# Two rows instead of nine: a narrower accumulator for the heads' sum in a decode step of sliding attention beside a gated unit

## The chip, the cores and the metric

The kernel runs on one core of a Trainium2 chip. The metric is the device time of one execution in microseconds; three runs of the kernel before gave a median of 377.54 us, from 377.41 to 377.73. The core has a matrix engine (TensorE, PE in the profile), a vector engine (VectorE, DVE), a scalar engine (ScalarE, ACT), a general engine (GpSimd, POOL) and a synchronisation engine (SyncE, SP), which here issues all DMA transfers. Sixteen DMA engines move the data between the chip's large memory and the on-chip memory SBUF. Matrix products land in a second small memory, PSUM.

## The reference

One token for each of two sequences (B = 2, D = 512) passes a layer norm, and the result feeds two branches whose outputs are added to the token: attention with 32 heads of width 128 over the last 2048 of 8192 cached positions, and a bilinear gated unit of width 1376.

```python
xn = _layernorm(x)
# attention, W = 2048
q = (xn @ wq).reshape(B, 1, 32, 128).transpose(0, 2, 1, 3)
scores = einsum("bhqd,bhkd->bhqk", q, k_cache[:, :, -W:]) * 128 ** -0.5
o = einsum("bhqk,bhkd->bhqd", softmax(scores), v_cache[:, :, -W:])
a = o.transpose(0, 2, 1, 3).reshape(B, 1, 4096) @ wo
# gated unit
b = ((xn @ w_gate) * (xn @ w_up)) @ w_down
return x + a + b
```

All values are float32. The keys, values and weights that are read make up nearly all of the 159.7 MB that the profile counts.

## The kernel before, in words

The host lays all large inputs out as one stream in the order of their use. The kernel reads it in 28 loads of up to 54 KB for each of the 128 partitions into three rotating buffers of SBUF (`step`, 55,296 bytes per partition), after one small load (`first`) with the token, two matrices of ones and zeros and the first head's query weights. The function `pump` issues a load as soon as a buffer is free; SP carries the loads out in this order and waits ahead of each for whatever used the buffer. An object `InOrder` ties each engine's instructions to the order in which the kernel names them.

For each head the keys lie with 16 positions of both sequences in each partition. DVE multiplies them with the broadcast query (`products`) and sums over the width (`sums`), POOL and ACT turn the sums into weights (`maxima`, `weights`), and PE multiplies the weights with the values (`weigh`), 16 columns wide in four column groups. ACT copies the result out, PE brings the head's output into a column for each sequence (`transpose`), and ACT scales it by the reciprocal of the sum into `oT`, a tile of 128 partitions by M columns.

The output product (`project_o`) then takes `oT` as the stationary operand and adds its product with the head's 128x512 slice of `wo` into the PSUM tile `acc`. The stationary operand has M = RB * (B - 1) + 1 = 9 columns, with the two sequences in columns 0 and 8 and zeros between (RB = 8). So the sums of the two sequences lie in rows 0 and 8 of `acc`. The gated unit uses the same layout: `gate` writes `hT` and `hX`, M columns wide at steps of RB, and `down` and `down_rest` add their products into the same rows.

Up to head 27 the whole 512 columns are one matmul. From head 28 on (`HF = H - 4`) the product is split into four column groups of 128 output columns each (`accumulate`), which land in rows 32g and 32g + 8 of a 128x128 view `acc_g`. Between the two, DVE copies the sum so far into SBUF (`acc_sb`, line 492), and `accumulate(carry, acc_sb)` brings it into the four groups by a matmul with the small matrix `carry`, which has ones at (0, 0) and (8, 8). At the very end DVE adds the token to the sums (line 529: `o_out` from `acc_g` and `x_nat`), and SP stores the 128x128 result, of which the host picks eight rows.

The token for that last addition comes by a load of 16 rows into `x_nat`, a 128x128 tile that a memset cleared ahead of it (lines 180 to 182), and `carry` comes by a load of 9 rows (line 185). Both are issued behind the first four loads of the stream. Memsets clear `oT`'s four copies (POOL, line 209), `hT` and `hX` (DVE, lines 391 and 394), since their columns between the two sequences must be zero.

Of the kernel before, what the change touches and what calls it, by code (L numbers as in the profile page):

```python
# [8 lines left out]
F32 = mybir.dt.float32  # L9
AF = mybir.ActivationFunctionType  # L10
ALU = mybir.AluOpType
# [5 lines left out]
P = 128  # L17
B, D, H, DH, SK, F = 2, 512, 32, 128, 8192, 1376
# [4 lines left out]
NFB = -(-F // FB)  # L23
NFC = F // P
FR = F - NFC * P
FH = [(0, 2 * FB), (2 * FB, F)]
LAG = 3
RB = 8
M = RB * (B - 1) + 1
OUT = P  # L30

CARRY = 72
HG = 4
GC = HG * DH
JG = J // 4
# [9 lines left out]
def blocks():  # L45

    def wd(n):
        return [("wd", i, D) for i in range(*WD[n])]

    def k(h):
        return [("k", h, CK)] + ([("wq", h, CP)] if h + HG < H else [])

    def v(h):  # L60
        return [("v", h, CK), ("wo", h, CO)]

    def gu(half):
        n = NC * (FH[half][1] - FH[half][0])
        return [("wg", half, n), ("wu", half, n)]

    units = []
    for h in range(LAG, H - 1):
        units += [k(h), v(h - LAG)]
    ones = [("pick", 0, 8 * B), ("rows", 0, NFB * B)]  # L70
    first = [("x", 0, B * NC)] + ones + [("w", 0, NC * DH)]
    loads = [[("w", 1, CQ - NC * DH)] + k(0) + k(1), gu(0) + k(2)]
    loads += [gu(1) + units[0] + units[1] + wd(0) + [("wr", 0, NS * P)]]
    loads += [sum(units[i : i + 3], []) for i in range(2, len(units), 3)]
    loads += [k(H - 1) + v(H - 1 - LAG) + wd(1)]
    out = [(("f", 0), first)] + [(("s", i), fields) for i, fields in enumerate(loads)]
    late, last = ("s", len(loads)), ("s", len(loads) + 1)
    out += [(late, v(H - 3)), (late, v(H - 2)), (last, [("v", H - 1, CK)])]
    out += [(last, [("wo", H - 1, CO)] + wd(2))]
    return out + [(last, wd(n)) for n in range(3, len(WD))]  # L80
# [33 lines left out]
def kernel(  # L114
    ctx: ExitStack,
    tc: tile.TileContext,
    x_rows: bass.AP,
    carry_rows: bass.AP,
    stream: bass.AP,
    out: bass.AP,  # L120
):
    nc = tc.nc
    pe, dve, act, sp = (InOrder(tc, e) for e in (nc.tensor, nc.vector, nc.scalar, nc.sync))
# [3 lines left out]
    const = ctx.enter_context(tc.tile_pool(name="const", bufs=1))  # L127
# [49 lines left out]
    pick = got["pick", 0][0].rearrange("p (r s b) -> p r s b", s=2, b=B)  # L177
    rows = got["rows", 0][0]

    x_nat = const.tile([P, P], F32, name="x_nat")  # L180
    dve.memset(x_nat, 0.0)
    sp.dma_start(x_nat[::RB, :], x_rows)

    carry = const.tile([P, CARRY], F32, name="carry")[:M, :M]
    sp.dma_start(carry, carry_rows)

    mean_w = const.tile([P, P], F32, name="mean_w")
    dve.memset(mean_w, 1.0 / D)
# [4 lines left out]
    dve.memset(acc_t, 0.0)  # L193
    acc, acc_g = acc_t[:M, :], acc_t[:, :P]

# [9 lines left out]


    oT_ring = [const.tile([P, M], F32, name=f"oT{i}") for i in range(4)]
    for t in oT_ring:
        nc.gpsimd.memset(t, 0.0)


    tr = ps_c.tile([P, 4 * P], F32, name="tr")
# [23 lines left out]
    q_ps, s_t, mm_t, p_t, sum_t, rec_t, o_sbs, oT = {}, {}, {}, {}, {}, {}, {}, {}  # L236
    n_acc = bank = 0

    def side(h):

        return int(h % 3 == 0)
# [43 lines left out]
    def sums(h):  # L285
        s_t[h] = small.tile([P, B, J], F32, name="s")
        dve.tensor_reduce(s_t[h], k_of(h), axis=AX.X, op=ALU.add)
        done("k", h)
# [28 lines left out]
    def accumulate(lhsT, rhs, last=False):  # L317
        nonlocal n_acc
        for g in range(4):
            pe.matmul(  # L320
                acc_g[32 * g : 32 * g + M, :], lhsT, rhs[:, g * P : (g + 1) * P],
                start=(n_acc == 0), stop=last,
# [23 lines left out]
    def transpose(heads, o_sb):  # L346
        d = tr[:, 8 + 4 * bank : 12 + 4 * bank]
        s0, s1 = side(heads[0]), side(heads[-1]) + 1
        dst = d.rearrange("p (s b) -> p s b", b=B)[:, s0:s1, :]
        for r in range(4):  # L350
            pe.matmul(
                dst, o_sb[:, r * DH : (r + 1) * DH], pick[:, r, s0:s1, :],
                start=(r == 0), stop=(r == 3),
            )
        for h in heads:
            rec = rec_t.pop(h)
            oT[h] = oT_ring[h % 4]
            for b in range(B):
                c = B * side(h) + b
                act.activation(  # L360
                    oT[h][:, RB * b : RB * b + 1], d[:, c : c + 1], AF.Copy,
                    scale=rec[:, b : b + 1],
                )

# [14 lines left out]
    def values(heads, busy=((), ())):  # L379
        o_sb = pv(heads)  # L380
        for n in busy[0]:
            keep_busy(n)
        transpose(heads, o_sb)
        for n in busy[1]:
            keep_busy(n)
        for h in heads:
            project_o(h)


    hT = const.tile([P, 4, NFB, M], F32, name="hT")  # L390
    dve.memset(hT, 0.0)

    hX = const.tile([P, NS, M], F32, name="hX")
    dve.memset(hX, 0.0)

    def project_gu(half):
        lo, hi = FH[half]
# [12 lines left out]
    def gate():  # L410
        g_sb = small.tile([P, FB], F32, name="o_sb", bufs=2)
        act.copy(g_sb, gu_ps[0])
        h_sb = small.tile([P, FB], F32, name="o_sb", bufs=2)
        dve.tensor_tensor(h_sb, g_sb, gu_ps[1], op=ALU.mult)
        for i in range(4):
            t = tr[:, P + i * P // 2 : P + i * P // 2 + NFB * B]
            pe.matmul(t, h_sb[:, i * P : (i + 1) * P], rows, start=True, stop=True)
            act.copy(hT[:, i, :, ::RB], t.rearrange("p (n b) -> p n b", b=B))
        for i in range(NS):
            t = tr[:, P + (2 * i + 1) * P // 4 : P + (2 * i + 1) * P // 4 + NFB * B]  # L420
            f = (NFC % 4) * P + i * FX - FR
            pe.matmul(t, h_sb[:, f : f + P], rows, start=True, stop=True)
            act.copy(hX[FR:, i, ::RB], t[FR:, (NFB - 1) * B :])

    def down(n):
        for c in range(*WD[n]):
# [51 lines left out]
    h = H - 2  # L478
# [10 lines left out]
    down(1)  # L489

    acc_sb = const.tile([M, D], F32, name="acc_sb")
    dve.tensor_copy(acc_sb, acc)
    sums(h + 1)
    transpose([HF], o_sb)
    keep_busy(256)
    accumulate(carry, acc_sb)
# [8 lines left out]
    o_sb = pv([H - 2])  # L505
    keep_busy(GC)
    transpose([H - 2], o_sb)
    keep_busy(256)
    project_o(H - 2)
# [3 lines left out]
    for k, t in enumerate((o_ps[bank], o_ps2)):  # L513
        for n in range(CK // FB):
            b, i = divmod(n, JG)
# [10 lines left out]
    down(3)  # L526
    down(4)
    o_out = const.tile([P, P], F32, name="o_out")
    dve.tensor_tensor(o_out, acc_g, x_nat, op=ALU.add)

    sp.dma_start(out, o_out[:OUT, :])

# [1 line left out]
def laid_out(x):  # L534

    import numpy as np

    a = x["A_x"].reshape(B, D)
    first = {
        kind: np.zeros((P, w), a.dtype) for kind, _, w in blocks()[0][1][:3]  # L540
    }
    carry = np.zeros((M, M), a.dtype)
    first["x"][:] = a.reshape(B, P, NC).transpose(1, 0, 2).reshape(P, B * NC)
    for b in range(B):
        for r in range(4):
            for s in range(2):
                first["pick"][8 * s + 4 * b + r :: 32, (2 * r + s) * B + b] = 1.0
        for n in range(NFB):
            first["rows"][32 * n + b, n * B + b] = 1.0
        carry[RB * b, RB * b] = 1.0  # L550
    cache = {
        kind: x[name][:, :, SK - W :, :].reshape(B, H, P, J * DH).transpose(1, 2, 0, 3)
        for kind, name in (("k", "A_k_cache"), ("v", "A_v_cache"))
    }
    wq = x["A_wq"].reshape(P, NC, H // HG, GC).transpose(2, 0, 1, 3)
    wo = x["A_wo"].reshape(H, P, D)
    gu = {
        kind: x[name].reshape(P, NC, F)
        for kind, name in (("wg", "B_w_gate"), ("wu", "B_w_up"))
    }  # L560
    wd = x["B_w_down"]
    rest = wd[NFC * P :].reshape(FR, NS + 1, P)

    def field(kind, i):
        if kind in first:
            return first[kind]
        if kind in ("k", "v"):
            return cache[kind][i].reshape(P, CK)
        if kind == "w":
            return (wq[0][:, :, DH:] if i else wq[0][:, :, :DH]).reshape(P, -1)  # L570
        if kind == "wq":
            return wq[i // HG + 1][:, i % HG, :]
        if kind == "wo":
            return wo[i]
        if kind == "wr":
            last = rest[:, NS, :].reshape(NS, FX, P).swapaxes(0, 1)
            return np.concatenate([rest[:, :NS, :], last]).reshape(P, NS * P)
        if kind == "wd":
            return wd[i * P : (i + 1) * P]
        return gu[kind][:, :, FH[i][0] : FH[i][1]].reshape(P, -1)  # L580

    parts = [
        np.concatenate([field(kind, i) for kind, i, _ in fields], axis=1).ravel()
        for _, fields in blocks()
    ]
    x_rows = np.zeros((D // P, 32 // RB, P), a.dtype)
    x_rows[:, :B] = a.reshape(B, D // P, P).transpose(1, 0, 2)
    return {
        "x_rows": x_rows.reshape(-1, P),
        "carry": carry,  # L590
        "stream": np.concatenate(parts),
    }

# [31 lines left out]
```

## Time and profile before

| what | value |
|---|---|
| median of three runs | 377.54 us (377.41 to 377.73) |
| span of the profiled execution, first to last instruction | 375.7 us |
| mean granted TensorE clock | 0.795 |
| PE, DVE, ACT, POOL busy | 68%, 78%, 16%, 7% |
| bytes moved by DMA, mean rate | 159.70 MB, 425 GB/s |

The profile is of one execution; it shows the span, and the time that the runs measure is somewhat longer, since it holds what lies around the first and the last instruction. Shares are of the span. In the rows of groups, the numbers behind the bar are busy time in all and the mean of one instruction, and behind the second bar the time in which the engine sat idle ahead of them and what ended it. Nearly all instructions carry line 98, the line of the helper that records their order, so that they are told apart by the names of their tiles. In the rows of the timeline the first number is the start in microseconds from the beginning of the span, the second the duration.

### The profile page before, as it was taken

How to read it: one execution, taken by the hardware profiler on the slowest of the kernel's cores; microseconds unless marked ns; L12 is line 12 of the kernel's file. 1: busy time of each engine (PE TensorE's matmuls, PEld its weight loads, DVE VectorE, ACT ScalarE, POOL GpSimd, SP SyncE). 2: the span in 40 equal slices, each digit the busy share in tenths (PEclk: the TensorE clock that was granted, in tenths of full speed). 3: DMA queues.
4: the chain of work that ended last, by engine and by line, in shares of the span. 5: the costliest groups of instructions: out<-in, count | busy, mean ns of one | idle time of the engine just before them, and what ended most of it. 6: DMA issues, size and time to landing. Idle time of an engine off the chain costs nothing.

```text
span 375.7 us, 2891 instructions
## 1 busy us (share of the span) xinstructions
PE 256.5 (68%) x1100; PEld 88.1 (23%) x1100; DVE 294.6 (78%) x147; ACT 58.7 (16%) x259; POOL 25.3 (7%) x78
## 2 busy tenths in 40 slices
PE   3396696986548487864848676485867639637996
PEld 3241122331112122211222211121212213021334
DVE  3299691998599499769949976994996799599960
ACT  1021001122020211201112020111202011121131
POOL 1001000000000000100000100000000000000010
PEclk9796988899696966859686786976669887556999
DMA  8999999899999999999999999999999999999995
GB/s 327 463 436 454 408 426 471 383 465 432 414 465 394 459 424 424 461 400 453 418 437 449 412 447 424 432 442 430 436 436 424 437 434 436 436 425 424 419 421 226
DMA packets 4382, 159.70 MB, mean 425 GB/s; under 512 B 514, under 2 KB 658, under 8 KB 1042
## 3 DMA queue, kind: packets, MB, share of 16 engines
q1 hardware_dynamic: 4370, 159.54, 98.5%
q8 instruction: 8, 0.13, 0.1%
q14 instruction: 4, 0.03, 0.0%
HBM read 159.47 MB, written 0.07 MB: 425 GB/s over the span
## 4 chain that ended last, share of the span: by engine, by line
DMA 62%; DVE 29%; PE 7%; ACT 1%; issue 0%; SPq 0%; DVEq 0%
DMA step<-in_stream_dram 62%; DVE s L98 14%; DVE step L98 14%; PE o_ps L98 3%; PE q L98 2%; PE acc L98 2%; PE tr L98 1%; DVE m L98 0%; ACT o_sb L98 0%; ACT oT L98 0%; SPq L98 0%; DVE rec L98 0%; DVE o_out L98 0%; DVEq L98 0%
## 5 line engine op out<-in xcount | busy, mean ns | idle before, releaser
L98 DVE TENSOR_TENSOR step<-step,q 128x4096 f32<-128x4096 f32 x31 | 136.6, 4408 | 53.3 <-DMA step<-in_stream_dram 53.3
L98 PE MATMUL q<-step,xnb 128*128 128x512 f32 (+1 forms) x128 | 92.7, 874 | 75.5 <-DMA step<-in_stream_dram 75.5
L98 DVE TENSOR_REDUCE s<-step 128x32 f32<-128x4096 f32 x32 | 141.4, 4419 | 1.1
L98 PE MATMUL o_ps<-step,p 128*16 128x512 f32 (+1 forms) x512 | 69.7, 682 | 10.3 <-DMA step<-in_stream_dram 10.3
L98 PEld LDWEIGHTS q<-step,xnb 128*128 128x128 f32 x128 | 32.2, 275 | 128.9 <-DMA step<-in_stream_dram 79.1
L98 PE MATMUL acc<-step,oT 128*9 128x512 f32 (+1 forms) x88 | 35.2, 554 | 9.3 <-ACT oT L98 8.1
L98 PE MATMUL tr<-first,o_sb 128*128 128x2 f32 (+2 forms) x198 | 27.6, 258 | 15.3 <-ACT o_sb L98 12.8
L98 ACT COPY o_sb<-o_ps 128x512 f32<-128x512 f32 (+1 forms) x24 | 13.8, 576 | 143.1 <-PE o_ps L98 143.1
L98 PEld LDWEIGHTS tr<-first,o_sb 128*128 128x128 f32 x198 | 25.5, 196 | 37.3 <-ACT o_sb L98 32.6
L295 POOL PARTITION_ALL_REDUCE mm<-m x32 | 11.3, 354 | 283.4 <-DVE rec L98 178.9
L98 PEld LDWEIGHTS o_ps<-step,p 128*16 128x16 f32 x512 | 13.5, 106 | 70.4 <-issue 55.2
L98 ACT ACTIVATE nm<-mm 128x2 f32<-128x2 f32 x32 | 6.5, 203 | 129.5 <-POOL mm L295 129.5
L98 ACT ACTIVATE p<-s,nm 128x16 f32<-128x16 f32 x64 | 19.2, 300 | 1.0
L98 ACT ACTIVATE oT<-tr,rec 128x1 f32<-128x1 f32 x64 | 12.2, 260 | 28.3 <-PE tr L98 28.3
L311 POOL PARTITION_ALL_REDUCE sum<-rs x32 | 12.7, 398 | 54.8 <-ACT p L98 54.8
L98 PE MATMUL o_ps<-step,xn 128*2 128x512 f32 (+1 forms) x48 | 12.9, 593 | 0.0
L98 ACT ACTIVATION_READ_ACCUMULATOR p<-s,nm 128x1 f32 x64 | 12.0, 187 | 0.0
L98 DVE TENSOR_TENSOR step<-step,tr 128x4096 f32<-128x4096 f32 x1 | 4.4, 4421 | 9.3 <-DMA step<-in_stream_dram 9.3
L98 PEld LDWEIGHTS acc<-step,oT 128*9 128x9 f32 x88 | 4.3, 91 | 19.5 <-ACT oT L98 13.1
L98 PE MATMUL q<-xnb,mean_w 128*128 128x512 f32 (+1 forms) x18 | 8.5, 563 | 0.0
L98 PE MATMUL acc<-step,hT 128*9 128x128 f32 (+2 forms) x58 | 7.9, 357 | 0.0
L98 DVE TENSOR_REDUCE m<-s 128x2 f32<-128x32 f32 x32 | 5.9, 186 | 1.1
(43 smaller groups left out, 36.5 us busy)
## 6 DMA issues: line engine op xcount, KB each, us to landing
step<-in_stream_dram SPq DMA_DIRECT2D x16, 6912.0 KB, 33.7
step<-in_stream_dram SPq DMA_DIRECT2D x2, 6400.0 KB, 32.6
step<-in_stream_dram SPq DMA_DIRECT2D x1, 6720.0 KB, 45.6
step<-in_stream_dram SPq DMA_DIRECT2D x1, 6656.0 KB, 28.9
step<-in_stream_dram SPq DMA_DIRECT2D x1, 5376.0 KB, 15.4
step<-in_stream_dram SPq DMA_DIRECT2D x1, 4864.0 KB, 30.1
step<-in_stream_dram SPq DMA_DIRECT2D x2, 2304.0 KB, 17.2
step<-in_stream_dram SPq DMA_DIRECT2D x1, 2048.0 KB, 15.9
```

The costliest lines, as they stand in the source:

```text
L98: made = call(*args, **kwargs)
L295: nc.gpsimd.partition_all_reduce(mm, m, P, bass_isa.ReduceOp.max)
L311: nc.gpsimd.partition_all_reduce(sum_t[h], rs, P, bass_isa.ReduceOp.add)
```

## The change

M becomes 2: the two sequences lie in rows 0 and 1 of `acc`, and in rows 32g and 32g + 1 of the four column groups. `oT`, `hT` and `hX` have two columns without gaps, and their memsets go. `x_nat` and `carry` become parts of one tile `x_own` of two rows, loaded at once: each row has a sequence's token (512 numbers) and a row of the 2x2 unit matrix. The token is added where the sum so far is carried over, on the 2x512 sum, and the last step on DVE is a copy.

```diff
-RB = 8
-M = RB * (B - 1) + 1
+M = B
@@
-    x_nat = const.tile([P, P], F32, name="x_nat")
-    dve.memset(x_nat, 0.0)
-    sp.dma_start(x_nat[::RB, :], x_rows)
-
-    carry = const.tile([P, CARRY], F32, name="carry")[:M, :M]
-    sp.dma_start(carry, carry_rows)
+    x_own = const.tile([P, D + M], F32, name="x_own")[:M, :]
+    sp.dma_start(x_own, x_rows)
+    x_nat, carry = x_own[:, :D], x_own[:, D:]
@@
     oT_ring = [const.tile([P, M], F32, name=f"oT{i}") for i in range(4)]
-    for t in oT_ring:
-        nc.gpsimd.memset(t, 0.0)
@@
-                    oT[h][:, RB * b : RB * b + 1], d[:, c : c + 1], AF.Copy,
+                    oT[h][:, b : b + 1], d[:, c : c + 1], AF.Copy,
@@
     hT = const.tile([P, 4, NFB, M], F32, name="hT")
-    dve.memset(hT, 0.0)
     hX = const.tile([P, NS, M], F32, name="hX")
-    dve.memset(hX, 0.0)
@@
-            act.copy(hT[:, i, :, ::RB], t.rearrange("p (n b) -> p n b", b=B))
+            act.copy(hT[:, i, :, :], t.rearrange("p (n b) -> p n b", b=B))
@@
-            act.copy(hX[FR:, i, ::RB], t[FR:, (NFB - 1) * B :])
+            act.copy(hX[FR:, i, :], t[FR:, (NFB - 1) * B :])
@@
-    dve.tensor_copy(acc_sb, acc)
+    dve.tensor_tensor(acc_sb, acc, x_nat, op=ALU.add)
@@
-    dve.tensor_tensor(o_out, acc_g, x_nat, op=ALU.add)
+    dve.tensor_copy(o_out, acc_g)
@@ on the host
-    x_rows = np.zeros((D // P, 32 // RB, P), a.dtype)
-    x_rows[:, :B] = a.reshape(B, D // P, P).transpose(1, 0, 2)
     return {
-        "x_rows": x_rows.reshape(-1, P),
-        "carry": carry,
+        "x_rows": np.concatenate([a, np.eye(M, dtype=a.dtype)], axis=1),
         "stream": np.concatenate(parts),
     }
```

More of the change, by code (lines that the diff above doesn't have):

```diff
@@ L27 @@
 LAG = 3
-RB = 8
-M = RB * (B - 1) + 1
+M = B
 OUT = P
-CARRY = 72
 HG = 4
@@ L117 @@
     x_rows: bass.AP,
-    carry_rows: bass.AP,
     stream: bass.AP,
@@ L541, in laid_out @@
     }
-    carry = np.zeros((M, M), a.dtype)
     first["x"][:] = a.reshape(B, P, NC).transpose(1, 0, 2).reshape(P, B * NC)
@@ L549, in laid_out @@
             first["rows"][32 * n + b, n * B + b] = 1.0
-        carry[RB * b, RB * b] = 1.0
     cache = {
@@ L623 @@
     y = r.results[0]["out_0_dram"]
-    return y[[32 * g + RB * b for b in range(B) for g in range(D // P)]].reshape(B, 1, D)
+    return y[[32 * g + b for b in range(B) for g in range(D // P)]].reshape(B, 1, D)
```

## The prediction

> **What bounds the kernel now.** I read the page first (engines, slices, queues, chain), then stretches of time, then the timeline of the head and of the tail.
>
> ```profile
> span 375.7 us, 2891 instructions
> PE 256.5 (68%) x1100; PEld 88.1 (23%) x1100; DVE 294.6 (78%) x147; ACT 58.7 (16%) x259; POOL 25.3 (7%) x78
> DMA  8999999899999999999999999999999999999995
> q1 hardware_dynamic: 4370, 159.54, 98.5%
> DMA 62%; DVE 29%; PE 7%; ACT 1%; issue 0%; SPq 0%; DVEq 0%
> step<-in_stream_dram SPq DMA_DIRECT2D x16, 6912.0 KB, 33.7
> first<-in_stream_dram SPq DMA_DIRECT2D x1, 271.0 KB, 2.9
> step<-in_stream_dram SPq DMA_DIRECT2D x1, 256.0 KB, 19.0
> ```
>
> No compute engine is busy over 78%, while one DMA queue is busy 98.5% of the span on all 16 engines. The chain of waits gives DVE 29%, but that is a habit of the view: it follows the buffer that the queue waited for, and the transfers went on beside it. The stretches of time tell whether they did; the last two columns are the busy share of the 16 DMA engines and the rate:
>
> ```profile
> 0.00:1.70 1.70, 0.00 (x0) 0.00 (x0) 0.78 (x4) 0.98 (x1) 1.17 (x14) 1.00 0.00 0
> 30.00:352.00 322.00, 220.43 (x842) 68.93 (x842) 266.69 (x119) 49.13 (x228) 21.83 (x58) 0.77 1.00 432
> 352.00:368.10 16.10, 15.79 (x120) 6.36 (x118) 10.66 (x10) 4.67 (x19) 1.50 (x4) 1.00 0.99 423
> 372.60:375.70 3.10, 0.35 (x8) 0.06 (x8) 0.29 (x1) 0.00 (x0) 0.00 (x0) 0.96 0.07 21
> ```
>
> For 322 us the share is 1.00 at 432 GB/s, although the TensorE clock was granted at 0.77 only. A load of 6912 KB (7.08 MB) at 432 GB/s takes 16.4 us but needs 33.7 us from issue to landing, so each load stands some 17 us in the queue behind another. That is the cover over everything PE, DVE, ACT and POOL do in the middle: an engine must be late by some 17 us before the queue runs dry. The end is set by the last rows of the stream and what follows them:
>
> ```profile
> 368.13 0.56 PEld L98 LDWEIGHTS o_ps<-step,p 128*16 128x16 f32 x16 [0.45 <-DMA step<-in_stream_dram]
> 372.55 0.12 PEld L98 LDWEIGHTS acc<-step,hT 128*9 128x9 f32 x8 [0.25 <-DMA step<-in_stream_dram]
> 373.02 0.29 DVE L98 TENSOR_TENSOR o_out<-acc,x_nat 128x128 f32<-128x128 f32 x1 [8.16 <-PE acc L98]
> 373.34 0.35 SPq L98 DMA_DIRECT2D out_dram<-o_out  x1
> ```
>
> PE sat idle 0.25 us for the last piece of weights, then 0.47 us until the sum was ready, 0.29 us on DVE, 0.03 to the issue, and 2.36 from there to the span's end. So the path is: 1.70 us before the first byte, the stream, and a tail of 3.15 us after 372.55. A change can move the time only by moving the stream's start, its rate or bytes, or one of those tail pieces. The span is 375.7; the three timed runs have their median 1.84 above it, and I carry that difference unchanged.
>
> **The change, part by part.**
>
> *Loads.* The head on SP and DVE:
>
> ```profile
> 0.82 0.17 DVE L98 MEMSET x_nat<- 128x128 f32 x1 [0.82 <-PEq L606]
> 1.15 1.37 SPq L98 DMA_DIRECT2D step<-in_stream_dram  x3
> 2.56 0.55 SPq L98 DMA_DIRECT2D x_nat<-in_x_rows_dram  x1
> 3.15 0.54 SPq L98 DMA_DIRECT2D carry<-in_carry_dram  x1
> 34.56 319.41 SPq L98 DMA_DIRECT2D step<-in_stream_dram  x25
> 3.64 0.16 DVE L98 TENSOR_REDUCE st<-first 128x2 f32<-128x8 f32 x1 [0.84 <-DMA first<-in_stream_dram]
> ```
>
> The stream's first four loads are issued before either small load, in both kernels. One issue of about 0.54 us goes from SP, which then has nothing to do from 3.69 to 34.56 us: worth 0. If that cover were gone it would be worth 0.54. The wait of the x load for a memset goes too, and nothing is queued behind it but the carry load. SP's later loads each wait for the load and the compute that used their buffer, in the same order; one load fewer only renumbers the completion semaphores.
>
> In the DMA queue itself the small loads stand between the third and the fourth buffer's load. Before: 16 rows of 512 B and 9 of 36 B; after: 2 rows of 2056 B. Prices come from stretches in which rows of one size only move (2168 B, 2048 B and 512 B, in this order):
>
> ```profile
> 2.32:2.82 0.50, 0.00 (x0) 0.00 (x0) 0.48 (x1) 0.00 (x0) 0.00 (x0) 1.00 0.84 330
> 371.36:371.76 0.40, 0.40 (x26) 0.38 (x19) 0.00 (x0) 0.24 (x2) 0.00 (x0) 1.00 0.48 184
> 374.18:374.45 0.27, 0.00 (x0) 0.00 (x0) 0.00 (x0) 0.00 (x0) 0.00 (x0) 1.00 0.78 231
> ```
>
> Rate over share, over 16 engines: 330/0.84/16 = 24.6 GB/s, so 88 ns for 2168 B; 184/0.48/16 = 24.0, so 85 ns for 2048 B; 231/0.78/16 = 18.5, so 28 ns for 512 B. An engine lost 28 to 56 ns before (a 36 B row costs between 0 and 28). After, an engine without a row loses nothing, and one with a row loses about 85. The stream ends with its slowest engine, which I can't name. Ends: -0.06 us (no row on that engine) and +0.14 (both rows on it: 170 - 28). I take -0.03, nearest to the 28 ns of the engines that had no 36 B row and now get nothing; that holds for most of the sixteen. The Trainium skill, page "DMA: Bandwidth & Descriptors", section "Why a DMA increments its semaphore by 16 and not by 1", says that a load is spread over the largest count up to 16 that divides its slowest dimension, so two rows would go to two engines; by it those two lose 85 ns and the sum would be +0.03 to +0.06 instead of -0.03. No run here shows it yet.
>
> *Memsets.* Removed:
>
> ```profile
> L209 POOL MEMSET oT<- 128x9 f32 x4 | 0.2, 107 | 0.0
> L98 DVE MEMSET hT<- 128x108 f32 x1 | 0.1, 148 | 0.0
> L98 DVE MEMSET hX<- 128x27 f32 x1 | 0.1, 81 | 0.0
> L98 DVE TENSOR_TENSOR step<-step,tr 128x4096 f32<-128x4096 f32 x1 | 4.4, 4421 | 9.3 <-DMA step<-in_stream_dram 9.3
> ```
>
> The x memset (0.17 us) lies ahead of 0.84 us idle for the first load, hT's and hX's (0.23) ahead of 9.3 us idle for the second, and POOL's 0.2 in front of nothing that is due before the first heads. Worth 0; without that cover 0.6 in all.
>
> *Width of the head sums, 9 columns to 2.* The matmul count stays. Rows for each width:
>
> ```profile
> L98 PE MATMUL acc<-step,oT 128*9 128x512 f32 x56 | 33.5, 714 | 9.3 <-ACT oT L98 8.1 <-ACT nm L98 1.2
> L98 PE MATMUL o_ps<-step,xn 128*2 128x512 f32 x32 | 8.0, 660 | 0.0
> L98 PEld LDWEIGHTS acc<-step,hT 128*9 128x9 f32 x56 | 1.9, 91 | 3.7 <-issue 3.4 <-DMA step<-in_stream_dram 0.3
> L98 PEld LDWEIGHTS o_ps<-step,xn 128*2 128x2 f32 x48 | 2.7, 88 | 11.6 <-issue 11.6
> ```
>
> A weight load is 3 ns shorter; the matmul means differ by 54 ns, but they come from stretches with other granted clocks, so the price of the width itself lies between 0 and 54. Ahead of the last load all of this is covered by the 17 us. After 372.55 there are eight pairs: four column groups at once, so at most two weight loads in a row, -0.01 to 0. ACT's copies into hT and hX and the scaled copies into oT keep their element counts and become contiguous; ACT is busy 16%: 0.
>
> *x joins the carried sum.* The 9x512 copy becomes an add of 2x512 from PSUM and SBUF:
>
> ```profile
> L98 DVE COPY acc_sb<-acc 9x512 f32<-9x512 f32 x1 | 0.7, 672 | 0.0
> L98 DVE TENSOR_TENSOR o_sb<-o_sb,o_ps 128x512 f32<-128x512 f32 x1 | 0.7, 678 | 0.0
> L98 DVE MEMSET x_nat<- x1: 165/165/165, 0.8 to 0.8; 128x128 f32 x1
> 363.30 0.13 PEld L98 LDWEIGHTS o_ps<-step,p 128*16 128x16 f32 x8 [0.46 <-DMA step<-in_stream_dram]
> ```
>
> By the add that the kernel already has, 678 against 672: +0.006 us at 356.80. Behind it on DVE stands the reduction of the last head, and PE waits for it with the carry matmuls; both then meet idle time for loads, 0.46 us at 363.30 and 0.45 at 368.13. The add now also waits for x, which comes before the fourth buffer's load, 300 us earlier. Worth 0, and 0.006 without the cover.
>
> *The last DVE step* loses an operand: add 292 ns to a copy from PSUM. The pair 672/678 says 6 ns; the outer ends are 165 (a memset of 128x128, which reads nothing) and 292. I take 0.286: -0.006, with -0.13 and 0 as ends. It lies wholly on the path.
>
> *Where the buffers lie.* The fixed tiles take 704 bytes more per partition, so in the built program's layout the three stream buffers start at 31424, 86720 and 142016 instead of 30720, 86016 and 141312 bytes: from multiples of 512 to odd multiples of 64. The stream is the bound, so even a few ns for each row would count: 28 loads x 128 rows / 16 engines = 224 rows per engine. The nearest row is the first load, which lies at 16512 (128 past a multiple of 256): its 2168 B took 88 ns against 85 for 2048 B at an aligned place, and 120 more bytes at 27 GB/s (432/16) are 4 ns. So nothing is charged for the place within the 1 to 2 ns of these figures. Ends: 0 and 7 ns per row; I take 0.
>
> Sum: -0.03 - 0.006 - 0.005 = -0.04 us; span 375.66, time **377.50**.
>
> **The rivals.**
>
> *A: the shifted buffers slow the stream (slower).* If an engine also moves the 192 bytes between the last 256-byte line and the start of each row, that is 192/27 = 7.1 ns x 224 = +1.6 us: 379.1. It decides from 3.4 ns a row (0.76 us). For it: the stream has no slack at all. Against it: the 88 ns of the first load, which would have been 93. The Trainium skill, page "DMA: Bandwidth & Descriptors", section "How a descriptor splits into AXI transactions", states for reads that a row not starting at a 256-byte boundary begins at the boundary below and pays for the unused bytes; applied to the writing side it would give the 379.1, and the first load's row does not bear it out. Chance 0.11.
>
> *B: the narrow width speeds up the path (faster).* If the buffers' release by PE were what paces the stream, the 64 matmuls of 512 columns would save up to 54 ns each, 3.4 us: 374.1. For it: the chain shows PE with 7%. Against it: share 1.00 at 432 GB/s over 322 us, which leaves nothing to speed up. Chance 0.05.
>
> *C: the merged load costs more than the two.* Both rows on the engine that ends last, +0.14 instead of -0.03: 377.67. For it: two long rows concentrate what sixteen short ones spread. It stays under what a measurement tells. Chance 0.15.
>
> **How the numbers follow.** My forecast has 0.67. It and C lie within 0.2% (0.76 us, about what a measurement of this kernel can tell from no change), 0.82 together. Slower: A and 0.01 for what I don't see, 0.12; faster: B and 0.01, 0.06. The forecast's own range: ends -0.2 and +0.2 and half the spread of the timed runs (0.16), 377.2 to 377.9. To leave no more than 2 in 10 out, with A at a part of its price, I reach to 377.0 and 378.2.
>
> **What would show it.** Right: 432 GB/s at share 1.00 in the middle; the first load of a buffer after the small one landing within 0.2 us of now; the last weights at 372.5; a last copy of 280 to 292 ns; the add at 670 to 685. A is seen in the rate of the middle stretch, below 431; B in narrower matmuls that end earlier and a last load that lands before 372 us; C in one engine's lag. The prediction is wrong if the rate moves, or if the tail after 372.55 is not 3.1 us.

## The result and the profile after

The changed kernel takes 378.19 us (median of 11 runs, 378.11 to 378.29) against 377.31 (11 runs) for the kernel before on the same chip: a ratio of 1.0020, 95% interval 1.0011 to 1.0029. It is slower by 0.88 us. My forecast was 377.50 and no change; the time lies just inside the stated range (377.0 to 378.2), outside the forecast's own 377.2 to 377.9, and the kernel got slower where I had forecast no change.

The page of the changed kernel, in the order of the prediction's first fence; the profiled execution took 378.21 us:

```profile
span 376.4 us, 2878 instructions
PE 256.4 (68%) x1100; PEld 88.4 (23%) x1100; DVE 294.4 (78%) x144; ACT 58.6 (16%) x259; POOL 25.2 (7%) x74
q1 hardware_dynamic: 4324, 159.54, 98.4%
step<-in_stream_dram SPq DMA_DIRECT2D x16, 6912.0 KB, 33.8
```

The engines' busy times hardly moved. The stretches of time (last columns: granted clock, DMA share, GB/s) say the same of the middle:

```profile
30.00:352.00 322.00, 218.05 (x839) 68.25 (x840) 266.38 (x119) 49.12 (x228) 21.84 (x58) 0.77 1.00 432
```

Both kernels read 432 GB/s here. That is no proof of equality: 0.88 us of 377 is 0.23%, and 0.23% of 432 is 1.0, which the whole numbers of this column can hide. The timeline shows what the rate can't. These are four of DVE's eleven multiplications that waited for a load, and for the changed kernel the tail from PE's last weights on; first the kernel before:

```profile
16.60 4.42 DVE L98 TENSOR_TENSOR step<-step,tr 128x4096 f32<-128x4096 f32 x1 [9.34 <-DMA step<-in_stream_dram]
97.97 4.42 DVE L98 TENSOR_TENSOR step<-step,q 128x4096 f32<-128x4096 f32 x1 [5.49 <-DMA step<-in_stream_dram]
228.41 4.42 DVE L98 TENSOR_TENSOR step<-step,q 128x4096 f32<-128x4096 f32 x1 [5.27 <-DMA step<-in_stream_dram]
325.15 4.42 DVE L98 TENSOR_TENSOR step<-step,q 128x4096 f32<-128x4096 f32 x1 [4.00 <-DMA step<-in_stream_dram]
```

and the changed kernel:

```profile
16.64 4.42 DVE L96 TENSOR_TENSOR step<-step,tr 128x4096 f32<-128x4096 f32 x1 [9.63 <-DMA step<-in_stream_dram]
98.04 4.42 DVE L96 TENSOR_TENSOR step<-step,q 128x4096 f32<-128x4096 f32 x1 [5.46 <-DMA step<-in_stream_dram]
228.76 4.42 DVE L96 TENSOR_TENSOR step<-step,q 128x4096 f32<-128x4096 f32 x1 [5.38 <-DMA step<-in_stream_dram]
325.60 4.42 DVE L96 TENSOR_TENSOR step<-step,q 128x4096 f32<-128x4096 f32 x1 [4.25 <-DMA step<-in_stream_dram]
373.20 0.11 PEld L96 LDWEIGHTS acc<-step,hT 128*2 128x2 f32 x8 [0.24 <-DMA step<-in_stream_dram]
373.67 0.29 DVE L96 COPY o_out<-acc 128x128 f32<-128x128 f32 x1 [7.99 <-PE acc L96]
373.99 0.35 SPq L96 DMA_DIRECT2D out_dram<-o_out  x1
```

The lag behind the kernel before is 0.04, 0.07, 0.35 and 0.45 us, and 0.65 at the last weights (372.55 before). So the loss builds up in the stream and was there before the tail began; each of these starts is from one execution, and those of two kernels of equal speed differ by up to 0.35 us (the first experiment). The tail from the last weights to the end is 3.2 us, as before. By 325 us all but 64 of each DMA engine's 224 rows are through (of the last eight loads seven are shorter): those 64 rows, 29%, fall into the last 47 us, an eighth of the time, and bring 0.20 of the 0.65. That hints at a lag that grows with rows rather than with time, but at this scatter it does not show it.

### The profile page after: what moved, and what is told of

Its sections match the earlier page's. It is cut to its first block, busy times and chain, and to the rows that moved or that the text cites. A ratio compares the mean times of both kernels' runs of the same rounds, so it can differ in the third digit from the quotient of the medians.

```text
span 376.4 us, 2878 instructions
## 1 busy us (share of the span) xinstructions
PE 256.4 (68%) x1100; PEld 88.4 (23%) x1100; DVE 294.4 (78%) x144; ACT 58.6 (16%) x259; POOL 25.2 (7%) x74
## 3 DMA queue, kind: packets, MB, share of 16 engines
q1 hardware_dynamic: 4324, 159.54, 98.4%
## 4 chain that ended last, share of the span: by engine, by line
DMA 62%; PE 20%; DVE 15%; ACT 1%; issue 1%; SPq 0%; DVEq 0%
DMA step<-in_stream_dram 62%; PE o_ps L96 8%; DVE s L96 7%; DVE step L96 7%; PE q L96 5%; PE acc L96 4%; PE tr L96 3%; ACT o_sb L96 0%; SPq L96 0%; ACT oT L96 0%; DVE o_sb L96 0%; ACT hT L96 0%; DVE m L96 0%; ACT hX L96 0%; DVE o_out L96 0%
## 5 line engine op out<-in xcount | busy, mean ns | idle before, releaser
L96 PE MATMUL acc<-step,oT 128*2 128x512 f32 (+1 forms) x88 | 35.0, 551 | 9.1 <-ACT oT L96 9.1
L96 PE MATMUL o_ps<-step,xn 128*2 128x512 f32 (+1 forms) x48 | 13.9, 615 | 0.0
L96 PEld LDWEIGHTS acc<-step,oT 128*2 128x2 f32 x88 | 3.8, 83 | 19.4 <-ACT oT L96 14.5
L96 DVE RECIPROCAL rec<-sum 128x2 f32<-128x2 f32 x32 | 5.0, 155 | 2.3 <-POOL sum L303 2.3
```

The source lines that it names most:

```text
L96: made = call(*args, **kwargs)
```

## The experiments

Theory D: the time goes into rows that are written to SBUF at places off some line, since the fixed tiles push the stream's buffers up by 704 bytes. Theory S: the stream lies at another place in the large memory, since the inputs ahead of it shrank. Theory L: the merged load, the narrower sums or another edit costs it.

**The changed kernel with its buffers moved back to multiples of 512.**

```diff
     hX = const.tile([P, NS, M], F32, name="hX")
+    pad = const.tile([P, 80], F32, name="pad")
+    nc.gpsimd.memset(pad[:, 0:1], 0.0)
```

> The changed kernel with 320 unused bytes ahead of the stream's buffers, so that these start at multiples of 512 again (31744, 87040, 142336). Theory D, the place of the buffers in SBUF slows the rows: back to the kernel before, 377.2 to 377.4 us, middle stretch back at 432 GB/s. Theory S, the place of the stream in the large memory moved because the inputs ahead of it shrank: still 378.1 to 378.3. Theory L, the merged load of two rows or another edit costs it: still 378.1 to 378.3.

Measured: 377.30 us against 377.40, ratio 0.9994 (0.9985 to 1.0004). All of the loss is gone, with every edit of the change in place. The same rows of its timeline:

```profile
16.45 4.42 DVE L96 TENSOR_TENSOR step<-step,tr 128x4096 f32<-128x4096 f32 x1 [9.46 <-DMA step<-in_stream_dram]
97.90 4.42 DVE L96 TENSOR_TENSOR step<-step,q 128x4096 f32<-128x4096 f32 x1 [5.70 <-DMA step<-in_stream_dram]
228.28 4.42 DVE L96 TENSOR_TENSOR step<-step,q 128x4096 f32<-128x4096 f32 x1 [5.33 <-DMA step<-in_stream_dram]
325.02 4.42 DVE L96 TENSOR_TENSOR step<-step,q 128x4096 f32<-128x4096 f32 x1 [3.99 <-DMA step<-in_stream_dram]
372.20 0.11 PEld L96 LDWEIGHTS acc<-step,hT 128*2 128x2 f32 x8 [0.19 <-DMA step<-in_stream_dram]
```

Against the kernel before they differ by -0.15, -0.07, -0.13 and -0.13, and -0.35 at the last weights; there is no growing delay.

**The kernel before with its buffers moved to where the changed kernel has them.**

```diff
     hX = const.tile([P, NS, M], F32, name="hX")
+    pad = const.tile([P, 176], F32, name="pad")
+    nc.gpsimd.memset(pad[:, 0:1], 0.0)
```

> The kernel before with 704 unused bytes ahead of the stream's buffers, so that these start where the changed kernel has them (31424, 86720, 142016); nothing else changed. Theory D: 378.1 to 378.3 us. Theories S and L: 377.2 to 377.5.

Measured: 378.16 us against 377.40, ratio 1.0022 (1.0012 to 1.0031). The unused bytes alone cost 0.76 us, within the intervals as much as the change (0.88). D stands; S and L fall.

**The reading side moved instead.** The kernel before, with 192 unused bytes at the head of the stream.

```diff
-    todo, at = [], 0
+    todo, at = [], 48
@@
-        "stream": np.concatenate(parts),
+        "stream": np.concatenate([np.zeros(48, a.dtype)] + parts),
```

> The kernel before with 192 unused bytes at the head of the stream in the large memory, so that every row that is read starts 192 bytes further; buffers where they were. Theory D in its plain form (only the writing side counts): 377.2 to 377.5 us. Theory S, or a rule that holds for reads that don't start at a 256-byte line: 224 rows x 7 ns at most, 378.1 to 379.0.

Measured: 377.53 us, ratio 1.0002 (0.9993 to 1.0012). The buffers stayed; the rows that are read start 192 bytes further, so that at least one of the two kernels reads off a 256-byte line. No cost shows: even the interval's upper end, 0.45 us, is below the 1.6 us that 192 unused bytes a row would take. (Where the stream's first byte lies in the large memory is not known. Had it been off the line, the shift could have saved bytes as well: 64 fewer a row would be 0.5 us, and the interval's lower end is -0.26.) The rule of the Trainium skill that I weighed ("DMA: Bandwidth & Descriptors", "How a descriptor splits into AXI transactions") is stated for reads; on the reading side this run does not bear it out, and where a cost was found it was on the writing side.

**How fine the line is.** The kernel before with 256, 128, 64 and 32 unused bytes in the same place (`pad` of 64, 32, 16 and 8 columns).

> The kernel before with 256 unused bytes ahead of the buffers, which then start at odd multiples of 256. Theory D with a line of 256 bytes: 377.2 to 377.4 us. Theory D with a line of 512 bytes: about 378.2. Theories S and L: 377.2 to 377.5.

> The kernel before with 128 unused bytes ahead of the buffers, which then start at odd multiples of 128. If any start off a 256-byte line costs the same (one more piece for each row): 378.1 to 378.3 us. If the cost goes by the bytes between the line below and the start (192 bytes cost 0.8 us): 0.55 us, 377.9. If the line is 128 bytes: 377.2 to 377.4.

> The same with 64 unused bytes; the buffers start at odd multiples of 64. Same cost for any start off the line: 378.1 to 378.3 us. Cost by the bytes below the start: 0.27 us, 377.6. If the cost goes by the bytes up to the next line (192 for this start, 64 for the changed kernel's): 2.4 us, 379.7.

> The kernel before with 32 unused bytes ahead of the buffers, which then start at odd multiples of 32. If any start off a 256-byte line costs the same: 378.1 to 378.3 us. If also a 64-byte step counts: above 378.5.

| buffers start behind a multiple of 256 by | us, and before beside it | ratio (95% interval) |
|---|---|---|
| 0 (shift 256) | 377.25, 377.40 | 0.9996 (0.9986 to 1.0005) |
| 32 | 378.44, 377.32 | 1.0029 (1.0018 to 1.0040) |
| 64 | 378.28, 377.29 | 1.0026 (1.0016 to 1.0035) |
| 128 | 378.07, 377.29 | 1.0020 (1.0010 to 1.0029) |
| 192 (shift 704) | 378.16, 377.40 | 1.0022 (1.0012 to 1.0031) |

The line is 256 bytes, not 128 or 512. Off it the cost is 0.8 to 1.1 us wherever the start lies, and the intervals overlap. A cost by the bytes below the start (a sixth of 0.8 us at 32) is out, and so is one by the bytes up to the next line (2.4 us at 64).

**Part of the loads shifted.** The kernel before with some fillings of a buffer written 192 bytes behind the start:

```diff
-                    tiles[key] = steps.tile([P, STEP], F32, name="step")
-                used[key] = 0
+                    tiles[key] = steps.tile([P, STEP + 64], F32, name="step")
+                used[key] = 48 if key[0] == "s" and key[1] % 2 else 0
```

> The kernel before with every second of the 26 first loads of a buffer written 192 bytes behind the buffer's start, the others at a multiple of 256. If each row that starts off the line pays for itself: half of the 0.8 us, 377.6 to 377.8. If one shifted load also upsets the next ones: 378.1 or more. If a mixed order costs nothing: 377.3.

The number of fillings in that text is wrong: there are 24, and the twelve shifted ones hold 15 of the 28 loads. Measured: 377.62 us against 377.29, ratio 1.0009 (1.0000 to 1.0019). At 15/28 of the changed kernel's loss, 0.47 us were to be expected; 0.33 came, with an interval from 0 to 0.7. That interval holds the expected share and no cost at all, so by the time alone the dose is not shown; the rows' own times below speak against a fixed price for each shifted row.

**By the row or by the byte.** The loads over 10,000 columns cut into two halves of each row, with the buffers in place and with the 704 bytes; the first was run twice.

```diff
-            sp.dma_start(tiles[key][:, c0:c1], src)
+            if c1 - c0 > 10000:
+                mid = c0 + (c1 - c0) // 128 * 64
+                sp.dma_start(tiles[key][:, c0:mid], src[:, : mid - c0])
+                sp.dma_start(tiles[key][:, mid:c1], src[:, mid - c0 :])
+            else:
+                sp.dma_start(tiles[key][:, c0:c1], src)
```

> The kernel before with its 21 longest loads cut in two halves of each row (both halves at multiples of 256): 168 rows more for each engine, 392 in place of 224. The profile's rows of 2048 and 4096 bytes put some 4 to 5 ns on each row: 0.7 to 0.8 us, and some 0.2 for 21 completions: 378.1 to 378.4 us. It is the base for the same cut with shifted buffers.

> The cut loads at aligned places once more, on the chip and beside the runs of the shifted ones: within 0.2 us of the first look at it.

> The cut loads with 704 unused bytes ahead of the buffers: every half row starts at an odd multiple of 64. If the shift costs a fixed time for each row, 0.85 x 392/224 = 1.5 us over the cut loads at aligned places. If it costs by the byte (or by the time that the stream runs): 0.85 us over them.

Measured: 378.31 and 378.32 us in place (ratios 1.0026 and 1.0027), 380.09 shifted (1.0071, 1.0056 to 1.0086). The 168 further rows for each engine cost 1.0 us even in place, as expected from the short rows. The shift on top costs 1.77 us by the medians and 1.45 between the profiled executions, whose last weights are these, in place first:

```profile
373.26 0.12 PEld L98 LDWEIGHTS acc<-step,hT 128*9 128x9 f32 x8 [0.21 <-DMA step<-in_stream_dram]
```

```profile
374.73 0.12 PEld L98 LDWEIGHTS acc<-step,hT 128*9 128x9 f32 x8 [0.23 <-DMA step<-in_stream_dram]
```

With 392 rows for each engine in place of 224, a fixed cost a row predicts 1.5, a cost by the byte 0.85. The difference of the two ratios (1.0071 and 1.0027, half widths 0.0015 and 0.0011) is 0.0044 with a half width of about 0.0019, or 1.0 to 2.4 us. So it goes by the row: 0.88/224 = 3.9 ns here, 1.77/392 = 4.5 ns there. The trace, which keeps the time of every row that a DMA engine moved, says so without this noise. In the load that begins at 323 us a whole row of 53,248 bytes took 1966.0 ns in place and 1969.8 shifted, on average; a half row took 987.0 and 990.9. Whole or half, it is 3.8 to 3.9 ns.

**The rows one by one.** The same records show where in the stream the cost arises. The table gives by how many ns the average row of a load took longer than the usual (median) row of that load in the kernel before; rows over 15 ns longer, which occur in every kernel, are left out.

| load begins at, us | bytes a row | before | changed kernel | every second filling shifted |
|---|---|---|---|---|
| 16 | 51,200 | 0.6 | 0.1 | 0.3 (shifted) |
| 31 | 53,760 | 1.8 | 1.2 | 1.0 (in place) |
| 177 | 55,296 | 0.1 | 4.5 | 0.3 (shifted) |
| 308 | 51,200 | 0.0 | 4.0 | 0.5 (shifted) |
| 350 | 18,432 | 0.0 | 3.9 | 0.2 (in place) |
| 366 | 8,192 | 0.0 | 4.5 | 1.9 (shifted) |
| 368 | 4,096 | 0.0 | 1.8 | 1.3 (shifted) |
| 370 | 2,048 | 0.0 | 0.8 | 0.9 (shifted) |

Summed over the rows of one engine this is 0.73 us in the changed kernel and 0.67 to 0.94 in the four shifted kernels of the table above, against 0.01 to 0.05 in the five kernels with all buffers in place. Three things stand out. In the first three loads a row off the line takes no longer; the excess comes over the loads that begin at 47, 63 and 79 us (0.7, 1.8 and 4.0 ns) and then stays. Rows of 4,096 bytes and less pay little even at the end. And where every second filling lies in place, the long rows of the shifted ones hardly pay: the sum is 0.11 us, so that most of the 0.33 us measured there, if it is real, is not explained. A long row pays some 4 ns among others that lie off the line as well, and not by its own place alone.

**What the other edits are worth.** The first experiment once more, with more rounds.

> The changed kernel with buffers at multiples of 512 once more, with more rounds: what its other edits are worth. The prediction's sum for them is -0.04 us, so the ratio to the kernel before is 0.9999; if the merged load costs as in rival C, +0.13, 1.0003. Neither is likely to stand clear of 1; a gain of over 0.2 us (below 0.9995) would say that something else was gained.

Measured: 377.38 us against 377.36, ratio 0.9997 (0.9988 to 1.0006). No gain and no loss can be told. It is as fast as the kernel before, so no run gives a version that beats it.

## Why the prediction was wrong

- *What bounds the kernel* was right: the stream sets the time, and nothing done on PE, DVE, ACT or POOL moved it. The signs that I named for a wrong prediction did not come up: the rate in the middle read 432 in both kernels, too coarse for rival A, and the tail stayed at 3.2 us. The last weights, at 373.20 us instead of 372.5, did show it.
- *Loads*: -0.03 taken, with -0.06 and +0.14 as ends. The two runs with aligned buffers lie at 0.9994 and 0.9997 with intervals of 0.001 around them; no part of the sum can be told apart at that size. The prices of single rows were right: the traces' records have 27 ns for 512 bytes and 84 for 2048 (28 and 85 taken), and 85 for each of the two new rows. The count behind it was right: the queue has 4324 packets in place of 4370, 46 fewer, which is 16 + 9 rows with a completion each (50) against 2 rows with one each (4). So the two rows went to two engines, as the Trainium skill has it ("DMA: Bandwidth & Descriptors", "Why a DMA increments its semaphore by 16 and not by 1"). Rival C's +0.13 (a ratio of 1.0003) lies inside both intervals and is neither shown nor excluded.
- *Memsets* were worth nothing: with them gone DVE sits idle 9.63 us for the second load in place of 9.34.
- *Width*: the rows of the changed kernel,

```profile
L96 PE MATMUL acc<-step,oT 128*2 128x512 f32 x56 | 33.4, 711 | 9.1 <-ACT oT L96 9.1
L96 PEld LDWEIGHTS acc<-step,hT 128*2 128x2 f32 x56 | 1.7, 84 | 3.0 <-issue 2.7 <-DMA step<-in_stream_dram 0.2
```

  say 711 ns in place of 714 and 84 in place of 91. The 54 ns between the two widths in the profile before belonged to their stretches, not to the width. Rival B was empty.
- *x joins the carried sum* and *the last DVE step* came out within 6 ns of their prices:

```profile
L96 DVE TENSOR_TENSOR acc_sb<-acc,x_own 2x512 f32<-2x512 f32 x1 | 0.7, 679 | 0.0
L96 DVE COPY o_out<-acc 128x128 f32<-128x128 f32 x1 | 0.3, 292 | 8.0 <-PE acc L96 8.0
```

  679 ns (678 taken), and 292 (286 taken): the copy from PSUM is no shorter than the add.
- *Where the buffers lie* is the step that failed: "So nothing is charged for the place within the 1 to 2 ns of these figures. Ends: 0 and 7 ns per row; I take 0." It measured 3.9 ns a row on average (0.88 us over 224), between the ends and above the 3.4 at which I had said that rival A decides. Rival A had the place right, the writing side of the stream's rows. Its price, by the bytes between the line and the start, was wrong: 192 such bytes cost 0.76 us instead of 1.6, and 32 cost no less. A got a chance of 0.11 because I let one row of the profile speak against it: the first load, which lies off the line and took no longer (88 ns, where my figures give 85 + 4 + 5 = 94 with the unused bytes, not 93). That row could not tell. It is short, and it lies in the head. In the changed kernel, where every row of the stream lies off the line, the usual rows of the first three loads take 1589, 1891 and 1985 ns as before, and even at the very end a row of 2048 bytes takes 84.8 ns in place of 84.0. The cost sits in the long rows from 63 to 79 us on, and the kernel before had none of those off the line. I had a term without slack, multiplied by 224, and a bound from a row of another length and another stretch; I should have taken the middle of the ends and given A about as much as no change.

What stays open is the mechanism: why the cost is absent in the first loads, why short rows pay less, and why long shifted rows among rows in place hardly pay. The time since the start alone does not set the beginning: with the rows cut in two and shifted, the third load, which begins at 31 us, already pays 3.0 ns a row. That a row off the line is cut into one more piece would fit a cost that is the same for every start, but not these three findings, and no run here looks inside a row.

## What to carry to other kernels

Where a stream of loads is the bound, the start of its buffers is part of the change, though no line of the diff names it: a fixed tile that grows or shrinks moves them. Place such buffers at multiples of 256 bytes in each partition, by a few unused bytes if need be, and look at their addresses before and after any edit of the fixed tiles. A rate in whole GB/s can't show 0.2%: compare the starts that waited for late loads, at several places along the stream, and the times of rows of one size. And a price of zero that is taken from one row holds for rows of its length and its part of the stream alone.

## What the runs showed of the hardware

- With all buffers of the stream off a 256-byte line in SBUF, the loads take 0.8 to 1.1 us longer over 224 rows for each engine, much the same for starts 32, 64, 128 and 192 bytes behind the line; 256 behind a multiple of 512 costs nothing (0.9996).
- In the changed kernel that is 3.1 to 4.6 ns for a row of 8,192 to 55,296 bytes in every load from 79 us on, 1.8 for 4,096 bytes, 0.8 for 2,048, and nothing in the first three loads. With every second filling in place, the rows of 8,192 bytes and more of the shifted ones took no more than 1.9 ns longer.
- 192 bytes of shift on the reading side, in the large memory, cost nothing that shows (1.0002; the rows of 18,432 bytes took 686 ns as before).
- Cutting rows of up to 55,296 bytes in two costs about 1.0 us over 168 more rows for each engine, some 6 ns for each, its share of the completions included.
